# All of batch 1's q turned by transfers, batch 0's k maximum spread by TensorE, the last block of out in 320 and 192 columns, and the queues listed anew

## The chip, the core and the metric

The kernel runs on one core of one Trainium2 chip. The time is the device time of one execution in microseconds (us), the median over runs; less is better. Five engines work beside each other, each through a queue of its own in a fixed order: TensorE (PE, with its weight loads as PEld), VectorE (DVE), ScalarE (ACT), GpSimd (POOL) and SyncE (SP). POOL and SP also issue transfers.

## What is computed

```python
# q, k, v: (8, 8, 576, 64) float32
q_s = softmax(q, axis=-1)            # with max subtracted, 1e-9 added to the sum
k_s = softmax(k, axis=2)             # over the 576 positions, in the same way
kv = np.einsum('bhsd,bhse->bhde', k_s, v)
attn = np.einsum('bhsd,bhde->bhse', q_s, kv)
x = attn.transpose(0, 2, 1, 3).reshape(4608, 512)
a = x @ w1                           # w1, w2: (512, 1024)
b = x @ w2
out = ((a * b) @ w3) @ w_out         # w3: (1024, 1024), w_out: (1024, 512)
```

## The kernel before

**Tiles.** The 128 partitions hold two heads of 64 rows each, and each row has nine tokens (j from 0 to 8); the free dimension holds four such pairs of heads, worked on in two halves (hp 0 and 1). Eight of the nine tokens make the 512 columns of one chunk of x; the ninth tokens of all eight batches are kept in `xtail` and make chunk 8. So there are nine chunks of 512 tokens.

**Folding.** w3 and w_out are multiplied first into one matrix W3O, in eight rows ft. For each ft: `w3t.ft` turns eight 128x128 blocks on TensorE, `w3T.ft` copies them out of PSUM, `pf.ft.0` and `pf.ft.1` are two halves of four matmuls each with the two halves of w_out, and `W3O.ft` copies the result out.

**Attention of batch b.** For k: `kmx` (the maximum over the nine tokens of each partition on DVE, as a tree of four instructions in the first four batches), then `cba`, `cbx`, `cb`, which spread the maximum over the partitions (a transpose of 32x32 blocks and a reduction on DVE, four small copies on ACT, a reduction and a transpose on DVE), then `ksub`, `kexp`, and on TensorE `kv` (with `vc`, a cast of v). `kve` and `kv2` divide by the sums. For q, in parts 0 (tokens 0 to 3) and 1 (tokens 4 to 8): `qmx`, `qsub`, `qexp`, `qsm`, `qeps`, `qrc`, `qn`. Then q has to be turned: on TensorE (`qt`, ten or eight blocks of 128x128, with `qT` to copy them out) or by a transposing transfer on SP (`qd`). Before, batch 0 is turned by TensorE, batch 1 in part 0 by a transfer and in part 1 by TensorE, and the others by transfers. `xm.b.h` and `xt.b` make x on TensorE, `xs` and `xts` copy it out.

**The chunk c.** `up.1` (with w2) and `up.0` (with w1) are eight matmuls of 256 columns, in chunks 0 and 1, or four of 512; `bs` casts the first product, `ab` on DVE multiplies the two; `down.c.tb` are eight matmuls with W3O, `os` copies out, `st` stores. The last block (`down.8.3`) is done in two pieces of columns, so that the end of the work is short.

**The order.** Nothing is scheduled by the compiler. `ORDER` is a list of all steps, and each engine's queue is that list with only its own steps; `PICKS` names the engine where there is a choice. `Plan.run` goes through it, and ties neighbouring steps of DVE and POOL that are marked with `port` to each other (`link`). PSUM has four banks in the ring `pab` (w3t, `up`), two in `po` (`pf`, `down`) and two in `att`; which ring an xm or xt takes, `XRING` says. `FILL` puts matmuls on zeros at the start. The loads in `HW` and `LATE` are issued by SP, those in `LOADS` by POOL, in that order, with a ninth load waiting for the first and so on; the first of `LATE` waits for w1's last quarter, the loads of a batch wait for their buffer, of which there are two.

```python
LOADS = [
    ("w3", 4), ("wo", 0), ("wo", 1), ("w3", 2), ("k", 0), ("w3", 0), ("w3", 3), ("w3", 5),
    ("w3", 1), ("v", 0), ("k", 1), ("w2", 0), ("q", 1, 0), ("w1", 0), ("w2", 1), ("w1", 1),
    ("w1", 2), ("w2", 2), ("k", 2), ("w2", 3), ("w1", 3), ("v", 1), ("q", 1, 1),
]
ROWS = [(0, 1), (1, 2), (2, 3), (3, 4), (4, 6), (6, 8)]   # rows of blocks in one load of w3
```

Of the kernel before, what the change touches and what calls it, by code (L numbers as in the profile page):

```python
# [927 lines left out]
```

## Time and profile before

| | before |
|---|---|
| median of 3 runs | 239.25 us (239.14 to 239.61) |
| the profiled execution | 239.21 us, span 237.4 us |
| TensorE busy | 230.1 us, 97% of the span |
| VectorE, ScalarE, GpSimd busy | 180.3, 121.7, 110.0 us |
| moved by transfers | 46.51 MB, 38.80 MB read from and 9.44 MB written to HBM |

All figures beside the time are of the one profiled execution, whose 239.21 us include 1.8 us around the span of its instructions. A busy TensorE isn't TensorE at its peak: its opening matmuls on zeros count as busy too. The rows of the profile name an instruction by its line in the code, the tile that it writes and those that it reads, and the shapes, with no number of the batch; a step is found by its place in the order.

### The profile page before, as it was taken

Reading aid. Unit: us, or ns where it says so; the run is one execution under the profiler, and the core shown is the slowest. Engines: PE = TensorE matmul, PEld = TensorE weight load, DVE = VectorE, ACT = ScalarE, POOL = GpSimd, SP = SyncE. Lnnn points to the kernel's source line nnn. Section 1 sums busy time; section 2 is a strip of 40 time slices with the busy share of each in tenths; the row PEclk is TensorE's granted clock in tenths of the full one; section 3 lists DMA queues with packets and bytes.
Section 4 is the critical chain, followed back from the end, with each engine's and each line's share of the span. In section 5 each row is a group of like instructions: output and inputs, shape, how many; then the busy total and the mean of one; then the engine's idle time right before and its main releaser. Section 6 shows DMA issues by size and latency. Waiting matters only on the chain.

```text
span 237.4 us, 4860 instructions
## 1 busy us (share of the span) xinstructions
PE 230.1 (97%) x1935; PEld 119.5 (50%) x1935; DVE 180.3 (76%) x277; ACT 121.7 (51%) x221; POOL 110.0 (46%) x73
## 2 busy tenths in 40 slices
...
GB/s 207 214 307 209 306 245 300 328 299 382 401 226 309 405 217 179 385 132 282 242 113 281 387 338 95 51 135 0 3 91 52 0 179 2 32 145 88 3 132 133
DMA packets 38742, 46.51 MB, mean 196 GB/s; under 512 B 17088, under 2 KB 22976, under 8 KB 38720
## 3 DMA queue, kind: packets, MB, share of 16 engines
...
HBM read 38.80 MB, written 9.44 MB: 203 GB/s over the span
## 4 chain that ended last, share of the span: by engine, by line
PE 81%; DMA 8%; DVE 5%; POOL 4%; issue 1%; ACT 0%; POOLq 0%; ACTq 0%
PE pab L784 46%; PE po L806 22%; DMA w<-in_moe_w_dram 6%; PE po L457 4%; PE po L821 3%; PE pkv L549 2%; DMA qT<-en 2%; PE xm L667 1%; DVE qm L582 1%; POOL k L524 1%; PE w3t L445 1%; POOL en L619 1%; POOL w L406 1%; DVE ab L799 1%; DVE kmx L498 1%
## 5 line engine op out<-in xcount | busy, mean ns | idle before, releaser
L784 PE MATMUL pab<-x,w1sb 128*128 128x512 f16 (+1 forms) x320 | 65.9, 337 | 0.4 <-DVE kmx L499 0.4
L784 PE MATMUL pab<-x,w2sb 128*128 128x512 f16 (+1 forms) x320 | 66.0, 337 | 0.0
L799 DVE TENSOR_TENSOR ab<-pab,bsb 128x512 f16<-128x512 f32 x72 | 48.6, 682 | 20.2 <-PE pab L784 13.6
L806 PE MATMUL po<-W3O,ab 128*128 128x512 f16 x256 | 58.9, 379 | 0.0
L784 PEld LDWEIGHTS <-w1sb 128*128 128x128 f16 x352 | 34.2, 98 | 28.5 <-DMA w1sb<-in_moe_w_dram 0.6
L784 PEld LDWEIGHTS <-w2sb 128*128 128x128 f16 x352 | 33.5, 98 | 27.5 <-issue 0.7
L325 ACT CAST bsb<-pab 128x512 f16<-128x512 f32 x46 | 26.8, 582 | 35.8 <-PE pab L784 34.6
L524 POOL TENSOR_TENSOR k<-k,cb 128x1152 f32<-128x1152 f32 x12 | 31.4, 2628 | 16.4 <-issue 5.1
L806 PEld LDWEIGHTS <-ab 128*128 128x128 f16 x256 | 24.5, 98 | 28.5 <-issue 0.4
L587 POOL TENSOR_TENSOR q<-q,qm 128x1024 f32<-128x1024 f32 (+1 forms) x14 | 29.5, 2125 | 13.1 <-DVE rc L573 5.4
L325 ACT COPY osb<-po 128x512 f32<-128x512 f32 (+1 forms) x25 | 14.3, 571 | 40.3 <-PE po L806 26.8
L619 POOL TENSOR_TENSOR en<-eq,qr 128x1024 f16<-128x1024 f16 (+1 forms) x13 | 27.2, 2106 | 10.5 <-DVE qr L612 10.4
L582 DVE TENSOR_REDUCE qm<-q 128x20 f32<-128x1280 f32 (+1 forms) x16 | 21.2, 1340 | 3.6 <-DMA q<-in_q_dram 3.6
L325 DVE CAST bsb<-pab 128x512 f16<-128x512 f32 x26 | 17.6, 677 | 6.8 <-PE pab L784 6.3
L600 DVE TENSOR_REDUCE qr<-eq 128x20 f32<-128x1280 f16 (+1 forms) x16 | 21.5, 1341 | 1.5 <-ACT eq L595 1.4
L595 ACT ACTIVATE eq<-q 128x1280 f16<-128x1280 f32 (+1 forms) x16 | 18.5, 1161 | 4.8 <-DVE q L587 3.9
L532 ACT ACTIVATE ek<-k 128x1152 f16<-128x1152 f32 x16 | 18.2, 1163 | 3.8 <-POOL k L524 3.8
L489 DVE TENSOR_REDUCE km<-k 128x128 f32<-128x1152 f32 x8 | 16.9, 2149 | 0.0
L457 PE MATMUL po<-wosb,w3T 128*128 128x512 f16 x64 | 15.3, 379 | 0.5 <-DMA wosb<-in_moe_w_out_dram 0.5
L325 DVE COPY osb<-po 128x512 f32<-128x512 f32 x12 | 8.3, 688 | 9.1 <-PE po L806 7.9
L329 ACT ACTIVATE x<-xm 128x512 f16<-128x512 f32 x18 | 10.3, 597 | 6.4 <-PE xm L667 6.2
L325 ACT CAST v<-v 128x1152 f16<-128x1152 f32 x9 | 10.3, 1148 | 0.3 <-DMA v<-in_v_dram 0.3
...
## 6 DMA issues: line engine op xcount, KB each, us to landing
...
q<-in_q_dram SPq DMA_DIRECT2D x5, 1152.0 KB, 7.7
v<-in_v_dram SPq DMA_DIRECT2D x5, 1152.0 KB, 8.9
k<-in_k_dram SPq DMA_DIRECT2D x4, 1152.0 KB, 10.1
k<-in_k_dram POOLq DMA_DIRECT2D x3, 1152.0 KB, 14.1
v<-in_v_dram POOLq DMA_DIRECT2D x1, 1152.0 KB, 13.9
v<-in_v_dram SPq DMA_DIRECT2D x2, 576.0 KB, 5.9
q<-in_q_dram SPq DMA_DIRECT2D x2, 576.0 KB, 7.7
```

The source lines that it names most:

```text
L325: return [(nc.scalar.copy if eng == "ACT" else engine[eng].tensor_copy)(out=out, in_=in_)]
L457: nc.tensor.matmul(st["pf", ft], lhsT=st["w3T", ft][:, gt, :], rhs=wosb[:, gt, :], start=(gt == 0), stop=(gt == N_FT - 1))
L524: return [engine[eng].tensor_tensor(out=kb[:, two(hp), :, :], in0=kb[:, two(hp), :, :], in1=st["cb", b][:, two(hp), None, :].broadcast_to( ...
L532: nc.scalar.activation(out=st["ek", b][:, hp, :, :].rearrange("p j (i d) -> p i j d", i=2), in_=kb[:, two(hp), :, :], func=AF.Exp)
L582: dve.tensor_reduce(out=st["qm", b][:, :, j], in_=qb[:, :, j, :], axis=AX.X, op=ALU.max)
L587: return [engine[eng].tensor_tensor(out=qb[:, :, j, :], in0=qb[:, :, j, :], in1=st["qm", b][:, :, j, None].broadcast_to([P, HH, n, D]), op ...
L595: nc.scalar.activation(out=st["eq", b, p], in_=qb[:, :, j, :], func=AF.Exp)
L600: dve.tensor_reduce(out=st["qr", b][:, :, slice(*PARTS[p])], in_=st["eq", b, p], axis=AX.X, op=ALU.add)
L619: return [engine[eng].tensor_tensor(out=st["en", b][:, j, :, :].rearrange("p j h d -> p h j d"), in0=st["eq", b, p], in1=st["qr", b][:, :, ...
L784: nc.tensor.matmul(st["p", one, c, sub, u][:, a * (t1 - t0):(a + 1) * (t1 - t0)], lhsT=w[:, ct, fb * P:(fb + 1) * P], rhs=x()[:, ct, t0:t1 ...
L799: dve.tensor_tensor(out=st["ab", c][:, nf * u:nf * u + nf, t0:t1], in0=cut(st["p", 0, c, sub, u]), in1=cut(st["bsb", c, sub, u]), op=ALU.mult)
L806: nc.tensor.matmul(st["po", c, tb], lhsT=st["ab", c][:, ft, tb * P:(tb + 1) * P], rhs=W3O[:, ft, :], start=(ft == 0), stop=(ft == N_FT - 1))
```

## The change

- `DMATS` 0 and an empty `DMATP`: part 1 of batch 1's q is also turned by a transfer (`qd.1.1`), so `qt.1.8`, `qt.1.16` and their copies `qT` go.
- `PEK = [0]`: in batch 0, `cba`, `cbx` and `cb` are replaced by `kT` (two fp32 transposes of 128x128 on TensorE), `kr` (a reduction on DVE from PSUM) and `kB` (four fp32 matmuls of 128 columns that spread the maximum over the partitions); `ksub.0`, always on DVE, reads the result from PSUM. `ident32` is an identity in fp32, copied by ACT.
- The last block of out is cut at column 320 instead of 256.
- From batch 3 on, `xm.b.0` takes two banks of `pab` instead of `att`.
- q of batch 7 is loaded in one transfer instead of two.
- `ORDER`, `PICKS`, `FILL`, `LOADS` and `LATE` are new lists. q's two normalisations of batch 0 (`qn.0.1`, `qn.0.0`) go from DVE to POOL.
- `CBX` and `KVE` keep what was there for the batches that they name.

The core of the diff, with the order as far as batch 2's first x:

```diff
@@ ORDER @@
-q.0.1 qmx.0.1 qsub.0.1 qexp.0.1 q.0.0 ident w3.4 w3t.5 qmx.0.0 qsm.0.1 wo.0 wo.1 w3.2 k.0 w3.0 w3.3
-w3.5 w3t.4 w3T.5 w3.1 w3T.4 qeps.0.1 qsub.0.0 qrc.0.1 qexp.0.0 qn.0.1 v.0 pf.5.0 pf.4.0 pf.5.1 w3t.2
-qsm.0.0 k.1 w2.0 w3T.2 W3O.5 q.1.0 qt.0.16 qt.0.8 qT.0.8 pf.4.1 qT.0.16 qeps.0.0 qrc.0.0 qn.0.0 w1.0
-pf.2.0 pf.2.1 w3t.0 W3O.2 W3O.4 w3T.0 qt.0.0 w3t.3 pf.0.0 w3T.3 w2.1 pf.0.1 pf.3.0 w3t.7 kmx.0.0
-cba.0 cbx.0 w1.1 pf.3.1 W3O.0 w3T.7 w3t.1 pf.7.0 w3t.6 w1.2 w2.2 cb.0 ksub.0.1 ksub.0.0 kexp.0.1
-kexp.0.0 pf.7.1 qT.0.0 kv.0 W3O.3 w3T.1 W3O.7 kve.0 pf.1.0 pf.1.1 w3T.6 kv2.0 xm.0.0 pf.6.0 pf.6.1
-xs.0.0.1 kmx.1.0 xs.0.0.0 xm.0.1 xs.0.1.0 xs.0.1.1 up.1.0.0.0 bs.0.0.0 xt.0 qmx.1.0 k.2 w2.3 cba.1
-cbx.1 up.0.0.0.0 up.1.0.1.0 up.0.0.1.0 W3O.1 bs.0.1.0 ab.0.0.0 up.1.0.0.1 up.0.0.0.1 w1.3 v.1
-qsub.1.0 qexp.1.0 q.1.1 q.2 xts.0.0 bs.0.0.1 up.1.0.1.1 ab.0.1.0 cb.1 up.0.0.1.1 up.1.0.0.2 qsm.1.0
-ksub.1.1 bs.0.1.1 ab.0.0.1 up.0.0.0.2 up.1.0.1.2 qeps.1.0 xts.0.1 qrc.1.0 qn.1.0 bs.0.0.2 ab.0.1.1
-ab.0.0.2 kmx.2.0 cba.2 bs.0.1.2 kexp.1.1 up.0.0.1.2 up.1.0.0.3 up.0.0.0.3 up.1.0.1.3 bs.0.0.3 W3O.6
-qd.1.0 cbx.2 ab.0.0.3 ksub.1.0 down.0.0 ab.0.1.2 cb.2 vc.1.1 kexp.1.0 vc.1.0 os.0.0 ksub.2.1
-up.0.0.1.3 down.0.1 ksub.2.0 qmx.1.1 qsub.1.1 kv.1 bs.0.1.3 os.0.1 kve.1 kexp.2.1 kexp.2.0 ab.0.1.3
-down.0.2 kv2.1 xm.1.0 down.0.3 xs.1.0.1 xs.1.0.0 up.1.1.0.0 up.0.1.0.0 up.1.1.0.1 qmx.2.1 qmx.2.0
-os.0.2 qsub.2.1 qexp.1.1 bs.1.0.0 qsm.1.1 qsub.2.0 v.2 up.0.1.0.1 up.1.1.0.2 qexp.2.1 ab.1.0.0
-vc.2.1 qeps.1.1 up.0.1.0.2 vc.2.0 qsm.2.1 bs.1.0.1 qexp.2.0 qeps.2.1 kv.2 qrc.1.1 bs.1.0.2 ab.1.0.1
-up.1.1.0.3 up.0.1.0.3 kve.2 ab.1.0.2 qn.1.1 qrc.2.1 kv2.2 qsm.2.0 qt.1.8 os.0.3 qt.1.16 bs.1.0.3
-ab.1.0.3 down.1.0 qeps.2.0 qn.2.1 qrc.2.0 qT.1.16 qT.1.8 xm.1.1 xs.1.1.0 k.3 down.1.1 st.0.0 st.0.1
-q.3 xs.1.1.1 xt.1 xts.1.0 k.4 qd.2.1 qmx.3.0 qmx.3.1 up.1.1.1.0 qn.2.0 bs.1.1.0 xts.1.1 qd.2.0
-kmx.3.0 cba.3 up.0.1.1.0 up.1.1.1.1 up.0.1.1.1 ab.1.1.0 xm.2.0 xs.2.0.0 bs.1.1.1 xs.2.0.1 cbx.3
-ab.1.1.1 cb.3 up.1.1.1.2 up.0.1.1.2 bs.1.1.2 xm.2.1 xs.2.1.0 xs.2.1.1 up.1.1.1.3 up.0.1.1.3 ab.1.1.2
...
+q.0.1 qmx.0.1 q.0.0 qmx.0.0 w3.2 w3.0 wo.0 wo.1 w3.4 qsub.0.1 qexp.0.1 k.0 ident w3t.2 w3T.2 w3t.0
+w3T.0 w3.3 w3.5 pf.2.0 qsm.0.1 qsub.0.0 qexp.0.0 qeps.0.1 qrc.0.1 pf.0.0 pf.2.1 pf.0.1 W3O.0 w3t.4
+q.1.0 qn.0.1 v.0 w3.1 k.1 qsm.0.0 qeps.0.0 qrc.0.0 W3O.2 ident32 qt.0.16 qt.0.8 w3t.5 w3T.4 pf.4.0
+pf.4.1 w3T.5 qT.0.8 W3O.4 pf.5.0 w3t.3 pf.5.1 kmx.0.0 kT.0 kr.0 qT.0.16 w3T.3 pf.3.0 kB.0 w3t.6
+W3O.5 w2.0 w1.0 w3T.6 w3t.7 qn.0.0 w1.1 qt.0.0 ksub.0.1 kexp.0.1 pf.3.1 pf.6.0 pf.6.1 ksub.0.0
+kexp.0.0 qT.0.0 qmx.1.0 kv.0 W3O.6 w3T.7 W3O.3 w3t.1 pf.7.0 kve.0 w2.1 w1.2 w2.2 k.2 qsub.1.0 w3T.1
+kv2.0 xm.0.0 xs.0.0.1 xs.0.0.0 pf.7.1 xm.0.1 pf.1.0 xs.0.1.0 xs.0.1.1 w2.3 w1.3 up.1.0.0.0 v.1 xt.0
+up.0.0.0.0 bs.0.0.0 q.1.1 kmx.1.0 cba.1 cbx.1 qexp.1.0 cb.1 ab.0.0.0 qsm.1.0 xts.0.1 pf.1.1 ksub.1.1
+ksub.1.0 up.1.0.1.0 bs.0.1.0 qeps.1.0 qrc.1.0 W3O.1 up.0.0.1.0 up.1.0.0.1 up.0.0.0.1 bs.0.0.1
+up.1.0.1.1 ab.0.1.0 up.0.0.1.1 ab.0.0.1 bs.0.1.1 up.1.0.0.2 up.0.0.0.2 up.1.0.1.2 kexp.1.0 ab.0.1.1
+bs.0.0.2 kmx.2.0 ab.0.0.2 cba.2 kexp.1.1 xts.0.0 W3O.7 q.2 qn.1.0 up.0.0.1.2 bs.0.1.2 ab.0.1.2
+up.1.0.0.3 up.0.0.0.3 up.1.0.1.3 up.0.0.1.3 bs.0.0.3 ab.0.0.3 down.0.0 cbx.2 cb.2 ksub.2.1 vc.1.0
+vc.1.1 qmx.1.1 bs.0.1.3 kexp.2.1 os.0.0 qd.1.0 kv.1 kve.1 kv2.1 ab.0.1.3 ksub.2.0 qmx.2.1 down.0.1
+down.0.2 os.0.1 qsub.1.1 qexp.1.1 qmx.2.0 xm.1.0 xs.1.0.1 down.0.3 xs.1.0.0 kexp.2.0 qsm.1.1
+qeps.1.1 qsub.2.1 up.1.1.0.0 up.0.1.0.0 up.1.1.0.1 up.0.1.0.1 bs.1.0.0 up.1.1.0.2 qexp.2.1 qsub.2.0
+qrc.1.1 ab.1.0.0 qsm.2.1 qexp.2.0 bs.1.0.1 v.2 k.3 qn.1.1 ab.1.0.1 vc.2.0 vc.2.1 qeps.2.1 qsm.2.0
+os.0.2 os.0.3 st.0.0 q.3 qd.1.1 st.0.1 st.0.2 qrc.2.1 up.0.1.0.2 up.1.1.0.3 kv.2 up.0.1.0.3 qeps.2.0
+bs.1.0.2 ab.1.0.2 qrc.2.0 bs.1.0.3 kve.2 ab.1.0.3 kv2.2 down.1.0 xm.1.1 qmx.3.0 qn.2.1 qn.2.0
+kmx.3.0 cba.3 xs.1.1.1 qsub.3.0 qd.2.1 down.1.1 qd.2.0 xs.1.1.0 qmx.3.1 xt.1 up.1.1.1.0 os.1.0
+os.1.1 xts.1.1 bs.1.1.0 up.0.1.1.0 xts.1.0 cbx.3 up.1.1.1.1 up.0.1.1.1 cb.3 bs.1.1.1 xm.2.0 xs.2.0.1
+qexp.3.0 xs.2.0.0 ab.1.1.0 up.1.1.1.2 up.0.1.1.2 bs.1.1.2 xm.2.1 ab.1.1.1 xs.2.1.0 xs.2.1.1 ab.1.1.2
...
 FILL = {
-    "begin": 17, "pf.5.0": 6,
+    "begin": 14, "pf.2.0": 8,
 }
...
 LOADS = [
-    ("w3", 4), ("wo", 0), ("wo", 1), ("w3", 2), ("k", 0), ("w3", 0), ("w3", 3), ("w3", 5),
-    ("w3", 1), ("v", 0), ("k", 1), ("w2", 0), ("q", 1, 0), ("w1", 0), ("w2", 1), ("w1", 1),
-    ("w1", 2), ("w2", 2), ("k", 2), ("w2", 3), ("w1", 3), ("v", 1), ("q", 1, 1),
+    ("w3", 2), ("w3", 0), ("wo", 0), ("wo", 1), ("w3", 4), ("k", 0), ("w3", 3), ("w3", 5), ("q",
+    1, 0), ("v", 0), ("w3", 1), ("k", 1), ("w2", 0), ("w1", 0), ("w1", 1), ("w2", 1), ("w1", 2),
+    ("w2", 2), ("k", 2), ("w2", 3), ("w1", 3), ("v", 1), ("q", 1, 1),
 ]
 
 
 LATE = [
-    ("q", 2), ("v", 2), ("k", 3), ("q", 3), ("k", 4), ("v", 3), ("q", 4), ("v", 4), ("q", 5),
-    ("k", 5), ("v", 5), ("q", 6), ("k", 6), ("v", 7), ("q", 7), ("v", 6), ("k", 7),
+    ("q", 2), ("v", 2), ("k", 3), ("q", 3), ("k", 4), ("q", 4), ("v", 3), ("v", 4), ("k", 5),
+    ("v", 5), ("q", 5), ("q", 6), ("v", 6), ("k", 6), ("q", 7), ("v", 7), ("k", 7),
 ]
 
 
...
     EPS = 1e-9
     PARTS = [(0, 4), (4, NJ)]
     WOS = 2
-    APART = [("q", 7), ("k", 7), ("v", 7)]
+    APART = [("k", 7), ("v", 7)]
     ROWS = [(0, 1), (1, 2), (2, 3), (3, 4), (4, 6), (6, 8)]
     COLS = [(0, 256), (256, 512), (512, 768), (768, 1024)]
 
...
+    ident32 = konst.tile([P, P], F32)
...
-    DMATS = 1
+    DMATS = 0
     VCASTS = 1
+    PEK = [0]
+    CBX = [1, 2, 3, 4, 5, 6, 7]
+    KVE = [0, 1, 2, 3, 4, 5, 6, 7]
...
-    DMATP = [(1, 0)]
+    DMATP = []
     XMS = 3
     DMAT = [[b > DMATS or (b, p) in DMATP for p in range(2)] for b in range(B)]
...
+    plan.add(("ident32",), "ACT", 0.28, lambda: nc.scalar.copy(out=ident32, in_=ident16), needs=[("ident",)],
+             lead=200.0)
...
+        def kT():
+            st["kT", b] = kbank("kT")
+            for n in range(NHP):
+                nc.tensor.transpose(st["kT", b][:, n, :], st["km", b].rearrange("p h d -> p (h d)")[
+                    :, n * P:(n + 1) * P], ident32)
+
+        def kr():
+            st["kr", b] = work.tile([P, NHP, G], F32, tag="kr", name="kr")
+            dve.tensor_reduce(out=st["kr", b], in_=st["kT", b].rearrange("p n (g r) -> p n g r", g=G),
+                              axis=AX.X, op=ALU.max)
+
+        def kB():
+            st["kB", b] = kbank("kB")
+            for n in range(NHP):
+                for gg in range(G):
+                    nc.tensor.matmul(st["kB", b][gg * HALF:(gg + 1) * HALF, n, :],
+                                     lhsT=st["kr", b][:, n, gg:gg + 1].broadcast_to([P, HALF]),
+                                     rhs=ident32, start=True, stop=True)
+            if not b:
+                st["cb", b] = st["kB", b].rearrange("p n (i d) -> p (n i) d", d=D)
+
...
+        kring = "att" if b else "pab"
+
+        def kbank(name):
+            if b:
+                return p_att([P, NHP, P], F32, name)
+            return pab_pool.tile([P, NHP, P], F32, tag="pab", name=name)
 
...
         def XRING(name):
             if name[1] < XMS:
                 return "att"
-            return "pab" if name[0] == "xt" else "po" if name[2] else "att"
+            return "po" if name[0] == "xm" and name[2] else "pab"
...
         kms = [("kmx", b, hp) for hp in hps if hp == 0 or not TREE[b]]
-        A(("cba", b), "DVE", 0.85, cba, kms)
-        A(("cbx", b), "ACT", 0.5, cbx, [("cba", b)])
-        A(("cb", b), "DVE", 0.62, cb, [("cbx", b)])
+        cbs, cbg = [("cb", b)], []
+        if b in PEK:
+            A(("kT", b), "PE", 0.45, kT, kms + [("ident32",)], takes=kring)
+            A(("kr", b), "DVE", 0.45, kr, [("kT", b)], gives=[("kT", b)])
+            A(("kB", b), "PE", 0.45, kB, [("kr", b)], takes=kring)
+            cbs, cbg = [("kB", b)], [("kB", b)]
+            if b:
+                A(("kc", b), {"ACT": (0.4, False), "DVE": (0.45, False)}, 0, kc, [("kB", b)], gives=[("kB", b)])
+                cbs, cbg = [("kc", b)], []
+        elif b in CBX:
+            A(("cba", b), "DVE", 0.89, cba, kms)
+            A(("cbx", b), "ACT", 0.83, lambda: cbx(True), [("cba", b)])
+            A(("cb", b), "DVE", 0.65, cbz, [("cbx", b)])
+        else:
+            A(("cb", b), "DVE", 2.25, cb, kms)
         for hp in hps:
-            A(("ksub", b, hp), pairs(2 * NJ * D, 2.63), 0, lambda eng, hp=hp: ksub(hp, eng), [("cb", b)])
+            how = {"DVE": (1.35, True)} if b == 0 and cbg else pairs(2 * NJ * D, 2.63)
+            A(("ksub", b, hp), how, 0, lambda eng, hp=hp: ksub(hp, eng), cbs, gives=cbg)
...
-                cuts = [0, C // 2, C] if tb == 3 else [0, C]
+                cuts = [0, 320, C] if tb == 3 else [0, C]
```

128 lines of the change are left out of this document (71 added, 57 removed), and 107 rows, old and new, of the table PICKS.

## The prediction

> **What bounds the kernel now.** I read the page first, then the busy times by stretch, then TensorE's own timeline, and last the issue and landing of the loads.
>
> ```profile
> span 237.4 us, 4860 instructions
> ```
>
> The profiled execution took 239.21 us, 1.8 more than its span, and the median of the runs is 239.25. I add my sum to 239.21, so it speaks of the median within 0.04 us.
>
> The stretches below are cut where TensorE's work changes: the first w3 block arrives at 8.87, the first `up` starts at 33.49, the last eighth of w1 is used at 45.79, batch 2's x starts at 73.37, and the last matmul is issued out at 234.36. Columns: stretch, its length, busy time (and instructions) of PE, PEld, DVE, ACT, POOL, then the granted clock, the DMA share and GB/s.
>
> ```profile
> 8.87:33.49 24.62, 23.52 (x276) 13.02 (x277) 20.51 (x31) 15.26 (x25) 8.75 (x12) 1.00 1.13 266
> 33.49:45.79 12.30, 11.94 (x116) 10.07 (x113) 11.83 (x20) 6.11 (x14) 8.62 (x6) 1.00 1.30 281
> 45.79:73.37 27.58, 27.10 (x346) 18.39 (x347) 25.96 (x42) 20.56 (x37) 20.93 (x10) 1.00 1.03 321
> 73.37:234.36 160.99, 160.98 (x1184) 75.81 (x1184) 117.76 (x178) 77.38 (x144) 65.96 (x32) 1.00 0.56 157
> 234.36:237.40 3.04, 0.00 (x0) 0.00 (x0) 0.00 (x0) 0.37 (x1) 0.00 (x0) 1.00 0.41 144
> ```
>
> After 73.37 TensorE is busy for 160.98 of 160.99 us: only less work or a shorter end gains there, and any new wait is paid in full. Before 73.37 the DMA share is over 1 throughout. So the question is how much of TensorE's work is left at 73.37. Here is its queue up to there (start, length, line, tiles, and the idle time before).
>
> ```profile
> 13.80 1.02 PE L457 MATMUL po<-wosb,w3T 128*128 128x512 f16 x4 [0.50 <-DMA wosb<-in_moe_w_out_dram]
> 15.05 0.71 PE L445 MATMUL w3t<-ident,w 128*128 128x128 f16 x8 [0.23 <-DMA w<-in_moe_w_dram]
> 15.60 0.72 PE L634 MATMUL qtp<-ident,en 128*128 128x128 f16 x10
> 16.16 2.75 PE L457 MATMUL po<-wosb,w3T 128*128 128x512 f16 x12
> ...
> 25.06 0.70 PE L445 MATMUL w3t<-ident,w 128*128 128x128 f16 x8
> 25.59 1.03 PE L457 MATMUL po<-wosb,w3T 128*128 128x512 f16 x4
> 26.46 0.65 PE L445 MATMUL w3t<-ident,w 128*128 128x128 f16 x8
> ...
> 27.90 0.78 PE L549 MATMUL pkv<-v,ek 64*64 64x64 f16 x72
> ...
> 29.14 1.90 PE L457 MATMUL po<-wosb,w3T 128*128 128x512 f16 x8
> 30.97 0.41 PE L667 MATMUL xm<-qT,kv 64*64 64x256 f16 x8
> 31.32 1.90 PE L457 MATMUL po<-wosb,w3T 128*128 128x512 f16 x8
> ...
> 34.66 1.05 PE L784 MATMUL pab<-x,w1sb 128*128 128x256 f16 x8
> ...
> 44.38 1.05 PE L784 MATMUL pab<-x,w2sb 128*128 128x256 f16 x8
> 45.79 1.05 PE L784 MATMUL pab<-x,w1sb 128*128 128x256 f16 x8 [0.36 <-DVE kmx L499]
> ...
> 64.50 0.72 PE L634 MATMUL qtp<-ident,en 128*128 128x128 f16 x10
> 65.06 1.89 PE L806 MATMUL po<-W3O,ab 128*128 128x512 f16 x8
> 66.88 0.41 PE L667 MATMUL xm<-qT,kv 64*64 64x256 f16 x8
> ...
> 73.37 0.41 PE L667 MATMUL xm<-qT,kv 64*64 64x512 f16 x4 [0.46 <-DMA qT<-en]
> ```
>
> Next, loads: for each its issue on POOL, then the row of the transfers' view around that issue, whose last number is the time to landing.
>
> ```profile
> 3.92 0.80 POOL L406 DMA_DIRECT2D k<-in_k_dram  x1
> k<-in_k_dram POOLq DMA_DIRECT2D x1, 1152.0 KB, 14.1
> 11.56 0.75 POOL L406 DMA_DIRECT2D v<-in_v_dram  x1 [1.90 <-DMA wosb<-in_moe_w_out_dram]
> v<-in_v_dram POOLq DMA_DIRECT2D x1, 576.0 KB, 16.2
> 19.36 0.74 POOL L406 DMA_DIRECT2D w1sb<-in_moe_w_dram  x1 [0.34 <-DMA w<-in_moe_w_dram]
> w1sb<-in_moe_w_dram POOLq DMA_DIRECT2D x1, 256.0 KB, 15.1
> 33.52 0.74 POOL L406 DMA_DIRECT2D w1sb<-in_moe_w_dram  x1 [0.62 <-DMA q<-in_q_dram]
> w1sb<-in_moe_w_dram POOLq DMA_DIRECT2D x1, 256.0 KB, 12.2
> ```
>
> So k of batch 0 lands at 18.0, v at 27.8, w1's first quarter at 34.46, and its last at 45.72. TensorE starts the first `up` on w1 at 34.66 and `up.0.0.0.3` at 45.79, 0.2 and 0.07 after those landings: both starts are set by loads, not by the engine that the second row names. The loads land in the order of their list.
>
> **Part by part: the start.** The new list holds the same fourteen loads up to w1's first quarter, and the same twenty-one up to its last, only in another order among themselves. At a DMA share above 1 I leave both landings at 34.46 and 45.72: no gain. POOL now issues them around q's two normalisations, so v of batch 0 is issued near 16 instead of 11.56; it landed 16.2 after its issue because others were ahead of it, some eight of these 16 us are slack, and I price this at nothing too, as I do the one filling matmul that goes before 13.80. What moves is the work of TensorE around them. In the new queue half a fold (`pf.1.1`, four matmuls) comes after `up.0.0.0.0`; all folds were done ahead of it before.
>
> When does the new queue reach `up.0.0.0.0`? The first two w3 pieces and wo come first, w3.4 fifth. From 13.80 to 15.05 one w3 piece of 256 KB arrives, 1.25 us; two such pieces ahead of w3.4 instead of one behind put it at 15.05 + 1.25 = 16.3. What is left from there to `up.1.0.0.0`, which TensorE does nearly without a pause:
> - six blocks of w3 turned, each with half a fold and the gap behind: 1.44 from 26.46 to 27.90, 8.64;
> - five more halves at 0.87 (25.59 to 26.46), 4.35;
> - eighteen blocks of q at 0.056 (ten from 15.60 to 16.16), 1.0;
> - kv.0 from 27.90 to 29.14, 1.24;
> - two xm at 0.35 (30.97 to 31.32) and three gaps of 0.1 (eight matmuls need 1.83 from 29.14 to 30.97, where 8 x 0.216 are 1.73), 1.0;
> - the new fp32 steps kT and kB, six matmuls of 128 columns, which no trace row shows: 0.34 if each costs an f16 block's 0.056, 1.35 at four times that. I take 0.9, nearer the upper end, as each value has twice the bytes.
>
> That is 17.1, and 33.4. Two waits come on top. k of batch 0 has one more w3 piece ahead, 19.2, and its maximum tree takes 2.9 on DVE (rows below), 22.1; TensorE is there at 21.9: 0.2. And `pf.4.0` follows its own eviction closely: 0.4, from 0 to 0.8. So `up.1.0.0.0` at 34.0, and with its 0.87 and xt's 0.3 `up.0.0.0.0` at 35.2, not 34.66. Then `pf.1.1` with its gap, 0.97, and twelve `up`, which took 10.6 from 34.66 to 45.26 (44.38 + 0.88): `up.0.0.0.3` at 46.8, **1.0 later**. If the load alone decides, 34.66 + 0.97 + 10.6 = 46.23, 0.44 later; with the upper prices 1.8 later.
>
> The Trainium skill, FP8 and Floating Point Precision, TensorE Precision Notes, says that true fp32 goes through the array four times; by it kT and kB come to about 1.35 and the sum to 0.45 more. No run here shows it.
>
> DVE and ACT get lighter in that stretch (two normalisations of q go to POOL, and four copies, two transposes and a reduction go away). I price this at nothing: TensorE was busy 23.52 of 24.62 us there, and the loads of w1 bound what follows.
>
> **q of batch 1 by transfers.** Ten blocks leave TensorE: 64.50 to 65.06, **-0.56**, and two evictions leave DVE and ACT, off the path. In their place SP issues one more transposing transfer, behind the load of q.3 and ahead of two stores and batch 2's transposes; k.4 moves behind those, to about 69, and is wanted by DVE only past 80 (nothing). It can start when POOL has normalised the second part.
>
> ```profile
> 60.55 1.14 POOL L325 CAST v<-v 128x1152 f16<-128x1152 f32 x1
> 61.82 6.50 POOL L619 TENSOR_TENSOR en<-eq,qr 128x1280 f16<-128x1280 f16 x3
> DMA to landing us min/median/max: 3.0/3.7/8.2
> ```
>
> The last row is of tile qT: how long such transfers took. The first of the three normalisations (2.3 us) ended at 64.1; the cast ahead of it now comes behind, so 63.0, and qT at 66.7 with the median of 3.7. TensorE reaches `xm.1.1` at 66.88 - 0.56 + 1.0 = 67.3. The cover is 0.6 us; with 8.2 it is 3.9 late. I take **+0.3**.
>
> By the Trainium skill, DMA: Bandwidth & Descriptors, Latency and other measured facts, a transposing DMA moves 261 GB/s, so ten blocks (327,680 bytes) would take an estimated 1.3 us and this term would be nothing. The trace's 3.0 at the least differs and decides.
>
> **The wait at 73.37** (0.46) is for batch 2's qT. TensorE comes 0.44 later and POOL's order ends at the same time: absorbed, **-0.46** (0 if SP's new order delays it as much).
>
> **DVE behind it.**
>
> ```profile
> 68.75 1.21 DVE L498 TENSOR_TENSOR kmx<-k 128x1024 f32<-128x1024 f32 x1
> 71.64 0.45 DVE L505 STREAM_TRANSPOSE kmq<-km 128x256 f32<-128x256 f32 x1
> 72.45 0.68 DVE L799 TENSOR_TENSOR ab<-pab,bsb 128x512 f16<-128x512 f32 x1
> ```
>
> That `ab.1.1.0` stands in the new order behind qmx.3.1, cb.3 and an eviction of xm.2.0 too, some 2.6 us more: it ends near 75, and `up.0.1.1.2`, which takes its bank, is reached near 74.5. **+0.3**, from 0 to 1.2.
>
> **Batches 3 to 7.** Their xm.b.0 takes two of the four pab banks, which `up` needs, where it had banks of its own. The full stretch shows no slack. Each could cost 0 to 0.4; I take **+0.2** in all.
>
> **The end.** Columns 320 and 192 leave TensorE the same columns, but the last eviction is shorter.
>
> ```profile
> L325 ACT COPY osb<-po 128x512 f32<-128x512 f32 x23 | 13.5, 588 | 39.5 <-PE po L806 26.8 <-PE po L821 10.1 <-issue 2.6
> L325 ACT COPY osb<-po 128x256 f32<-128x256 f32 x2 | 0.7, 372 | 0.8 <-PE po L821 0.8
> ```
>
> By these two, 192 columns take about 318 ns, 0.05 less, and the store is a quarter smaller: **-0.1**, 0 to -0.2.
>
> Sum: 1.0 - 0.56 + 0.3 - 0.46 + 0.3 + 0.2 - 0.1 = +0.7. **Forecast 239.9 us**, its own range 239.3 to 240.8.
>
> **Rivals.**
> - *The start stays bound by the load* (faster). If TensorE is at `up.0.0.0.0` by 34.66, as cheap fp32 steps and hidden evictions would allow, and no new wait shows: 0.44 - 0.56 - 0.46 - 0.1 = -0.7, **238.5**. For it: DVE and ACT are lighter in the start. Against it: 17 us of work between 16.3 and 34. It decides from 0.5 us less than my walk. Chance 0.30.
> - *No new wait, but the late start*: 1.0 - 0.56 - 0.46 - 0.1 = -0.1, **239.1**. Chance 0.15.
> - *The new transposing transfer comes late* (much slower). If it takes the 8.2 us of the longest so far, xm.1.1 waits 3.9: 1.0 - 0.56 + 3.9 - 0.46 - 0.1 = +3.8, **243.0**. For it: q.3 is just ahead of it in the same queue. Against it: the median is 3.7. Chance 0.08.
> - *The shared banks bite* in each of five batches at 0.4: 0.7 + 1.8, **241.7**. Chance 0.05.
>
> The forecast has 0.42, of which a quarter falls within 0.2%. That bound, 0.48 us, is about what a measurement of this kernel can tell from no change: 238.77 to 239.73. So faster 0.31, same 0.22, slower 0.47. The range 238.2 to 241.5 leaves out the last two rivals and the outermost of the first.
>
> **What would show it.** In the new profile: `up.0.0.0.0` at 35.2 and `up.0.0.0.3` at 46.8; kT and kB near 0.9 us together; no idle ahead of xm.2.0, at most 0.3 ahead of xm.1.1, some ahead of `up.0.1.1.2`; TensorE full from there on; a final copy near 0.32. Wrong would be: `up.0.0.0.0` at 34.7 (the first rival), w1's last quarter landing at another time than 45.7, or idle TensorE of over 1 us after 75.

## The result, and the profile after

| | before | after | ratio, 95% interval |
|---|---|---|---|
| median of 7 runs each, in turns | 239.61 us | 240.04 us | 1.0025, 1.0013 to 1.0036 |
| the changed kernel once more, on the chip of the last experiments | 239.54 us | 239.90 us | 1.0015, 1.0001 to 1.0028 |
| the profiled execution | 239.21 us, span 237.4 | 240.33 us, span 238.3 | |

The changed kernel is slower by 0.43 us, or by 0.36 us the second time, against the bound of 0.48 us that the prediction named. The two profiled executions lie 1.12 us apart, more than the medians: before's is 0.40 under its median of seven, after's 0.29 over its own. Some 0.2 us of the 1.12 lie outside the span (1.8 us around it before, 2.0 after). What follows names differences between two executions, and each of them carries some 0.3 us of that.

The busy times of the changed kernel by stretch, cut at the same events as before: the first w3 block on TensorE, the first `up`, `up.0.0.0.3`, batch 2's x, the last matmul. Columns as in the prediction.

```profile
7.90:33.78 25.88, 23.91 (x284) 13.46 (x285) 19.32 (x28) 15.24 (x22) 15.19 (x16) 1.00 1.14 264
33.78:46.97 13.19, 12.68 (x118) 10.64 (x117) 10.58 (x19) 8.65 (x19) 7.66 (x6) 1.00 1.27 295
46.97:74.18 27.21, 26.76 (x337) 17.85 (x337) 25.80 (x42) 19.46 (x39) 20.36 (x11) 1.00 1.08 280
74.18:235.30 161.12, 161.12 (x1184) 75.00 (x1184) 114.27 (x171) 74.94 (x142) 69.09 (x34) 1.00 0.58 164
235.30:238.30 3.00, 0.00 (x0) 0.00 (x0) 0.00 (x0) 0.32 (x1) 0.00 (x0) 0.88 0.42 149
```

The full stage is as full as it was and 0.13 us longer. Nearly all of the difference within the span arises ahead of 74.18. TensorE's timeline of the changed kernel there:

```profile
22.52 0.44 PE L547 MATMUL kT<-ident,km 128*128 128x128 f32 x2 [0.23 <-DVE km L513]
22.79 1.03 PE L469 MATMUL po<-wosb,w3T 128*128 128x512 f16 x4
23.75 0.66 PE L559 MATMUL kB<-ident,kr 128*64 128x128 f32 x8
24.34 1.19 PE L457 MATMUL w3t<-ident,w 128*128 128x128 f16 x16
...
34.93 1.05 PE L857 MATMUL pab<-x,w1sb 128*128 128x256 f16 x8
35.82 1.03 PE L469 MATMUL po<-wosb,w3T 128*128 128x512 f16 x4
...
45.41 1.04 PE L857 MATMUL pab<-x,w2sb 128*128 128x256 f16 x8
46.97 1.03 PE L857 MATMUL pab<-x,w1sb 128*128 128x256 f16 x8 [0.52 <-ACT bsb L335]
...
56.04 1.90 PE L879 MATMUL po<-W3O,ab 128*128 128x512 f16 x8
58.07 1.03 PE L857 MATMUL pab<-x,w2sb 128*128 128x256 f16 x8
...
67.82 0.41 PE L725 MATMUL xm<-qT,kv 64*64 64x256 f16 x8
...
74.18 0.41 PE L725 MATMUL xm<-qT,kv 64*64 64x512 f16 x4 [0.33 <-DMA qT<-en]
```

From start to next start, kT takes 0.27 us and kB 0.59. `up.0.0.0.0` starts at 34.93, `up.0.0.0.3` at 46.97, 1.18 later than before, batch 1's x (`xm.1.1`) at 67.82, 0.94 later, batch 2's (`xm.2.0`) at 74.18, 0.81 later. Three waits stand in it.

The first, at 46.97: eight matmuls of 256 columns take 0.87 (44.54 to 45.41 in the same view), so TensorE was there at 45.41 + 0.87 = 46.28. The last quarter of w1 was issued at 33.59 and landed 12.5 later, 46.09. What was missing was a PSUM bank. The row names a cast on ACT, `bs.0.1.2`. ACT's timeline has it behind two exponentials of k and two other evictions; it is the first of the two in the last row, took 0.60 and ended at 46.92, 0.05 ahead of the matmul:

```profile
43.08 1.17 ACT L586 ACTIVATE ek<-k 128x1152 f16<-128x1152 f32 x1 [1.25 <-DMA w2sb<-in_moe_w_dram]
44.16 0.57 ACT L335 CAST bsb<-pab 128x512 f16<-128x512 f32 x1
44.62 1.16 ACT L586 ACTIVATE ek<-k 128x1152 f16<-128x1152 f32 x1
45.69 0.27 ACT L339 ACTIVATE xtail<-xt 128x128 f16<-128x128 f32 x1
45.84 0.60 ACT L339 ACTIVATE W3O<-po 128x512 f16<-128x512 f32 x1
46.32 1.08 ACT L335 CAST bsb<-pab 128x512 f16<-128x512 f32 x2
```

The bank that had been in use longest is the one that `ab.0.0.2` empties. DVE's timeline has that step behind the maximum tree of batch 2, and it ended at 46.50 + 0.69 = 47.19, after the matmul had begun:

```profile
43.56 1.23 DVE L510 TENSOR_TENSOR kmx<-k 128x1024 f32<-128x1024 f32 x1 [0.68 <-DMA k<-in_k_dram]
...
46.01 0.43 DVE L513 TENSOR_TENSOR km<-kmx,k 128x256 f32<-128x256 f32 x1
46.50 0.69 DVE L872 TENSOR_TENSOR ab<-pab,bsb 128x512 f16<-128x512 f32 x1
```

Before, `ab.0.0.2` came ahead of this tree. So TensorE waits 0.69 us for a bank from two engines that were called lighter: DVE frees none before 47.19, as its tree waits for a load of k, and ACT, with its queue full, frees the next at 46.92.

The second, at 58.07: `down.0.3` ends at 56.04 + 1.73 = 57.77. ACT has an exponential of q (`qexp.1.1`) ahead of the eviction of x (`xs.1.0.0`), and it waits for POOL's subtraction:

```profile
56.26 1.27 ACT L653 ACTIVATE eq<-q 128x1280 f16<-128x1280 f32 x1 [1.60 <-POOL q L645]
57.44 0.58 ACT L339 ACTIVATE x<-xm 128x512 f16<-128x512 f32 x1
```

The third, at 74.18, is for batch 2's transposing transfers. POOL's and SP's timelines, and the end of the chain of waits there:

```profile
64.19 4.20 POOL L677 TENSOR_TENSOR en<-eq,qr 128x1280 f16<-128x1280 f16 x2 [0.40 <-DVE qr L670]
```

```profile
62.72 1.80 SPq L700 DMA_TRANSPOSE qT<-en  x1
64.56 3.20 SPq L905 DMA_DIRECT2D out_dram<-osb  x4
67.87 2.84 SPq L700 DMA_TRANSPOSE qT<-en  x2
```

```profile
68.40 0.78 SPq L700
69.18 0.05 issue
69.23 0.02 SPq L700
69.25 0.03 issue
69.28 4.76 DMA qT<-en
74.04 0.14 issue
74.18 0.41 PE xm L725 x4
```

POOL had the second source ready at 68.39, as before (68.32). But SP's queue holds the new transfer `qd.1.1` and four stores first and needs 5 us to issue them (62.72 to 67.76), so the transfer that `xm.2.0` needs went out at 69.28, 0.9 behind its source. It landed 4.76 us after that; before, the same transfer went out at 68.35 and landed 4.89 later.

### The profile page after: what moved, and what is told of

It reads as the page before. It is cut to its first block, busy times and chain, and to the rows that moved or that the text cites. A ratio compares the mean times of both kernels' runs of the same rounds, so it can differ in the third digit from the quotient of the medians.

```text
span 238.3 us, 4853 instructions
## 1 busy us (share of the span) xinstructions
PE 229.6 (96%) x1934; PEld 118.7 (50%) x1934; DVE 172.6 (72%) x263; ACT 119.9 (50%) x222; POOL 118.1 (50%) x78
## 2 busy tenths in 40 slices
DMA packets 40038, 46.84 MB, mean 197 GB/s; under 512 B 18384, under 2 KB 24272, under 8 KB 40016
## 4 chain that ended last, share of the span: by engine, by line
PE 72%; DMA 14%; POOL 4%; DVE 3%; issue 3%; ACT 2%; SPq 0%; DVEq 0%; POOLq 0%; ACTq 0%
PE pab L857 46%; PE po L879 19%; DMA k<-in_k_dram 12%; PE po L894 3%; DMA qT<-en 2%; PE pkv L603 2%; POOL k L578 1%; DVE kmx L510 1%; POOL q L645 1%; PE pab L725 1%; POOL w L416 1%; POOL en L677 1%; DVE kmx L511 1%; ACT eq L653 1%; PE po L725 1%
## 5 line engine op out<-in xcount | busy, mean ns | idle before, releaser
L335 ACT CAST bsb<-pab 128x512 f16<-128x512 f32 x49 | 28.3, 584 | 53.9 <-PE pab L857 53.7
L677 POOL TENSOR_TENSOR en<-eq,qr 128x1280 f16<-128x1280 f16 (+1 forms) x15 | 31.9, 2137 | 24.7 <-DVE qr L670 15.5
L335 ACT COPY osb<-po 128x512 f32<-128x512 f32 (+1 forms) x28 | 15.9, 578 | 14.5 <-PE po L879 8.1
L335 DVE CAST bsb<-pab 128x512 f16<-128x512 f32 x23 | 15.7, 683 | 4.4 <-PE pab L857 3.9
L335 DVE COPY osb<-po 128x512 f32<-128x512 f32 (+1 forms) x9 | 6.0, 664 | 15.6 <-PE po L879 10.8
L469 PEld LDWEIGHTS <-w3T 128*128 128x128 f16 x64 | 5.9, 98 | 7.0 <-issue 1.7
L335 POOL CAST v<-v 128x1152 f16<-128x1152 f32 x8 | 9.1, 1148 | 0.0
```

The source lines that it names most:

```text
L335: return [(nc.scalar.copy if eng == "ACT" else engine[eng].tensor_copy)(out=out, in_=in_)]
L469: nc.tensor.matmul(st["pf", ft], lhsT=st["w3T", ft][:, gt, :], rhs=wosb[:, gt, :], start=(gt == 0), stop=(gt == N_FT - 1))
L677: return [engine[eng].tensor_tensor(out=st["en", b][:, j, :, :].rearrange("p j h d -> p h j d"), in0=st["eq", b, p], in1=st["qr", b][:, :, ...
```

## The experiments

Two theories were set against each other. A: what ends last ahead of the full stage is the chain to batch 2's q, and TensorE's delays ahead of it are free. B: TensorE's queue, each wait paid in full. All ran in five rounds beside the kernel before, which had medians of 239.50 (e), 239.48 (f1 to f4) and 239.54 (the last four).

| run | median us | ratio to before, 95% | xm.2.0 at |
|---|---|---|---|
| e1_no_bank_wait | 239.62 | 1.0006, 0.9995 to 1.0017 | 73.59 |
| e2_stores_behind | 242.71 | 1.0136, 1.0109 to 1.0163 | 75.24 |
| e4_blocks_back | 241.36 | 1.0080, 1.0067 to 1.0093 | 75.42 |
| e5_no_fp32 | 239.67 | 1.0008, 0.9998 to 1.0019 | 73.49 |
| f1_x_first | 240.13 | 1.0027, 1.0018 to 1.0036 | 74.21 |
| f2_three_waits | 239.37 | 0.9995, 0.9984 to 1.0007 | 73.17 |
| f3_q2_sooner | 239.38 | 1.0001, 0.9989 to 1.0013 | 72.91 |
| f4_no_fp32 | 239.78 | 1.0014, 1.0003 to 1.0025 | 74.47 |
| c_again | 239.90 | 1.0015, 1.0001 to 1.0028 | 74.33 |
| f5_att_banks | 241.75 | 1.0094, 1.0075 to 1.0112 | 74.09 |
| f6_blocks_uncovered | 239.54 | 1.0004, 0.9993 to 1.0015 | 73.53 |
| g_best | 240.81 | 1.0068, 1.0042 to 1.0095 | 73.01 |

**e1: the bank wait.**

```diff
-bs.0.0.2 kmx.2.0 ab.0.0.2 cba.2 kexp.1.1 ... up.0.0.1.2 bs.0.1.2 ab.0.1.2
-up.1.0.0.3 up.0.0.0.3 up.1.0.1.3 up.0.0.1.3 bs.0.0.3 ab.0.0.3 down.0.0 cbx.2
+bs.0.0.2 kmx.2.0 ab.0.0.2 kmy.2 cba.2 kexp.1.1 ... up.0.0.1.2 bs.0.1.2
+up.1.0.0.3 up.0.0.0.3 bs.0.0.3 ab.0.0.3 up.1.0.1.3 down.0.0 ab.0.1.2 up.0.0.1.3 cbx.2
...
+            one = [top(out=t, in0=kb[:, :, 0:4, :], in1=kb[:, :, 4:8, :], op=ALU.max)]
+            return one if b == 2 else one + kmy()
```

> The changed kernel, with the wait ahead of up.0.0.0.3 taken away: batch 2's maximum tree (kmx.2.0) is cut behind its first instruction and ab.0.0.2 goes between the two pieces; ab.0.0.3 and down.0.0 go ahead of ab.0.1.2 and up.0.0.1.3, so that no later wait takes its place. Theory A (what ends last ahead of the full stage is the second transposing transfer of batch 2's q, landed at 74.04; TensorE's own delays ahead of it are free): up.0.0.0.3 starts at 46.3 instead of 46.97, but xm.2.0 still at 74.1 to 74.3 behind a wait of about 1.0 instead of 0.33, and the median stays at 240.0. Theory B (TensorE's queue: each of its waits is paid in full): xm.2.0 near 73.5, the median 239.4.

No idle time is left ahead of `up.0.0.0.3`, which starts at 46.15, though ACT's cast of `bs.0.1.2` ends as late as it did (46.84): DVE's order is enough. The second wait took most of it back, `up.1.1.0.0` is only 0.18 earlier:

```profile
57.89 1.03 PE L865 MATMUL pab<-x,w2sb 128*128 128x256 f16 x8 [0.72 <-ACT x L339]
...
73.59 0.41 PE L730 MATMUL xm<-qT,kv 64*64 64x512 f16 x4
```

The median fell by 0.19% against the changed kernel's first ratio, 0.4 us, and by 0.09% against its second, 0.2 us, between A's nothing and B's 0.6. A named the wrong place: it was ACT's order at 57.9 that gave the gain back, not the transfer at 74. In this execution SP was through its stores sooner (both transposing transfers out from 67.07) and no wait for qT shows; `xm.2.0` is where B had it, the median is not, so neither theory held as it stood.

**e2: the stores behind the transfers.** Only SP's queue changes.

```diff
-os.0.2 os.0.3 st.0.0 q.3 qd.1.1 st.0.1 st.0.2 qrc.2.1
+os.0.2 os.0.3 st.0.0 q.3 qd.1.1 qrc.2.1
...
-qd.2.1 down.1.1 qd.2.0 xs.1.1.0
+qd.2.1 down.1.1 qd.2.0 st.0.1 st.0.2 xs.1.1.0
```

> The changed kernel, with the four stores of blocks 0.1 and 0.2 moved behind the two transposing transfers of batch 2's q in SP's queue, nothing else. In the changed kernel SP issued the first of the two at 67.87, behind those stores (its source was normalised near 66.5), and the second at 69.28 (its source was ready at 68.39). Theory A (that transfer ends last): the second is issued near 68.5, lands near 73.3, xm.2.0 starts at 73.85 with no wait, the median goes to 239.7. Theory B (a transposing transfer's time is set by the traffic beside it, not by its issue): landing stays near 74.0, the median at 240.0.

Both missed: 2.7 us slower than the changed kernel. ACT's and TensorE's timelines:

```profile
74.42 0.58 ACT L335 COPY osb<-po 128x512 f32<-128x512 f32 x1 [4.76 <-DMA out_dram<-osb]
```

```profile
75.24 0.40 PE L725 MATMUL xm<-qT,kv 64*64 64x512 f16 x2 [1.57 <-ACT xtail L339]
```

There are four output buffers. The eviction `os.1.1` needs that of `st.0.1`; it stood 4.76 us on ACT, and the evictions of xtail, which free the banks of `xm.2.0`, stood behind it. The edit made a wait of its own, so the median says nothing on the transfers. The trace does: with the stores behind, the second transfer went out at 68.28, as A said, and landed after 3.11 us, at 71.38, where A had 73.3 and B 74.0. Of the stores only `st.0.2` can move, as f2 does.

**e4: the ten blocks back on TensorE.** The copies go to DVE (`qT.1.16`) and ACT (`qT.1.8`).

```diff
-    DMATS = 0
-    DMATP = []
+    DMATS = 1
+    DMATP = [(1, 0)]
...
-st.0.0 q.3 qd.1.1 st.0.1
+st.0.0 q.3 st.0.1
...
-ab.1.0.3 kv2.2 down.1.0 xm.1.1 qmx.3.0
+ab.1.0.3 kv2.2 qt.1.8 qt.1.16 down.1.0 qT.1.16 qT.1.8 xm.1.1 qmx.3.0
```

> The changed kernel, with part 1 of batch 1's q turned by TensorE again as before (ten blocks of 128x128 ahead of down.1.0, copied out by DVE and ACT), and its transposing transfer gone. Theory A (TensorE has only 0.33 us of cover ahead of batch 2's x): the 0.56 us of blocks move xm.2.0 to 74.4, the median is 240.2 to 240.3. Theory B (every block counts): 240.6. Theory C (the added transfer disturbs the others in its queue): batch 2's transfers land earlier without it and the median is at or below 240.0.

```profile
67.07 0.73 PE L692 MATMUL qtp<-ident,en 128*128 128x128 f16 x10 [1.27 <-DVE kv L633]
```

The blocks take their banks from att, which in this order `kv.2` holds until DVE's `kv2.2`: 1.27 of waiting and 0.57 of blocks. That is again the edit's own wait; f6 mends it. C is borne out as far as the transfers go: without the added one, batch 2's second went out at 68.16 and landed at 71.26.

**e5: no fp32 on TensorE.** The three old steps take the place of the three new ones.

```diff
-    PEK = [0]
-    CBX = [1, 2, 3, 4, 5, 6, 7]
+    PEK = []
+    CBX = [0, 1, 2, 3, 4, 5, 6, 7]
...
-pf.5.1 kmx.0.0 kT.0 kr.0 qT.0.16 w3T.3 pf.3.0 kB.0 w3t.6 W3O.5 w2.0
+pf.5.1 kmx.0.0 cba.0 qT.0.16 w3T.3 pf.3.0 w3t.6 W3O.5 cbx.0 cb.0 w2.0
```

> The changed kernel, with batch 0's maximum of k spread by DVE and ACT as before (cba, cbx, cb) and no fp32 steps on TensorE. Theory A: TensorE loses 0.86 us of work ahead of the first up, which then starts with w1's first quarter near 34.6 instead of 34.93; what follows is held by the bank of up.0.0.0.3 at 46.97 and by batch 2's q at 74.04, so xm.2.0 stays at 74.1 to 74.2 and the median at 240.0. Theory B (the start is TensorE's work): up.0.0.0.0 near 34.1, the median 239.2 to 239.5. Theory C (the maximum comes late without TensorE): kv.0 waits up to 1 us and the median is above 240.3.

`up.0.0.0.0` came at 35.15, not sooner: kv.0 waits for its exponential and starts 21.02 us after the first w3 block, where it took 20.60 in the changed kernel. B is out: the 0.86 us of TensorE's work that went away came back as waiting (0.63 of it ahead of kv.0), since the maximum comes later on DVE and ACT in this order. That is C's mechanism, though not C's median, and A's 34.6 missed. The median is nevertheless 0.17% lower than the changed kernel's first ratio and 0.07% lower than its second; this execution, with SP's list unchanged, shows no wait at `xm.2.0`, where A had it held by batch 2's q.

**f1: x ahead of the exponential on ACT.** One step moves.

```diff
-qsub.1.1 qexp.1.1 qmx.2.0 xm.1.0 xs.1.0.1 down.0.3 xs.1.0.0 kexp.2.0
+qsub.1.1 qmx.2.0 xm.1.0 xs.1.0.1 down.0.3 xs.1.0.0 qexp.1.1 kexp.2.0
```

> The changed kernel, with ACT's exponential of batch 1's q, part 1 (qexp.1.1), moved behind xs.1.0.0, as before the change; nothing else. In the changed kernel and in three of the four runs so far ACT did this exponential first, which waits for POOL's subtraction near 56.0 to 56.2, and TensorE's up.1.1.0.0 started at 57.8 to 58.1 whatever came ahead of it. Theory A (this order on ACT is a wall that hides what the start loses): up.1.1.0.0 follows down.0.3 without a gap, near 57.7 to 57.8 and 0.1 to 0.3 earlier, the median 239.8 to 239.9. Theory B (the exponential is itself on the chain to batch 2's q): qn.1.1 ends 0.2 to 0.4 later, xm.2.0 waits for it, the median at 240.0 to 240.3.

```profile
74.21 0.41 PE L725 MATMUL xm<-qT,kv 64*64 64x512 f16 x4 [0.71 <-DMA qT<-en]
```

`up.1.1.0.0` came without a gap (57.76), as A said, and the whole of it was lost at 74.21, so the median is B's. POOL waited 0.81 for batch 2's reciprocal where it had waited 0.40.

**f2: all three waits.** The edits of e1 and f1, and:

```diff
-st.0.0 q.3 qd.1.1 st.0.1 st.0.2 qrc.2.1
+st.0.0 q.3 qd.1.1 st.0.1 qrc.2.1
...
-qd.2.1 down.1.1 qd.2.0 xs.1.1.0
+qd.2.1 down.1.1 qd.2.0 st.0.2 xs.1.1.0
```

> The kernel without the bank wait (e1), with xs.1.0.0 ahead of qexp.1.1 too, and with the two stores of block 0.2 alone moved behind batch 2's two transposing transfers (not those of block 0.1, whose buffer the next block needs). Without them up.1.1.0.0 would start near 57.2 (0.72 earlier than in e1) and xm.1.1 near 66.9. Theory A (the transfers of q then end last): a wait of 0.2 to 0.5 shows ahead of xm.1.1 or xm.2.0, since qT of part 1 lands near 67.2 and that of batch 2 near 73.2; xm.2.0 at 73.1 to 73.3, the median 239.3. Theory B (TensorE's queue alone): no wait, xm.2.0 at 72.9, the median 238.9.

```profile
66.50 3.10 SPq L705 DMA_TRANSPOSE qT<-en  x2
```

```profile
73.17 0.41 PE L730 MATMUL xm<-qT,kv 64*64 64x512 f16 x4
```

With two of the four stores in front, the pair went out from 66.50 instead of 67.87, and the second transfer, out at 68.37, landed after 3.1 us. TensorE reached batch 2's x 1.0 us sooner than in the changed kernel and found it there: B in the trace. The median gained 0.3% on the changed kernel's first ratio, 0.7 us (0.2%, 0.5 us, on its second), and stands where A put it. It is the kernel before's time. The profiled execution is 0.58 above this median, and shows one place where it lost time later: batch 3's x waited for a transposing transfer too, which landed 6.9 us after its issue.

```profile
92.77 0.41 PE L730 MATMUL pab<-qT,kv 64*64 64x512 f16 x4 [0.34 <-DMA qT<-en]
```

**f3: batch 2's normalisation sooner.** On top of f2:

```diff
-ab.1.0.1 vc.2.0 vc.2.1 qeps.2.1 qsm.2.0 os.0.2
+ab.1.0.1 vc.2.0 qeps.2.1 vc.2.1 qrc.2.1 qsm.2.0 os.0.2
```

> The kernel of f2, with batch 2's normalisation brought forward: qeps.2.1 ahead of the cast vc.2.1 on ACT and qrc.2.1 ahead of qsm.2.0 on DVE, which takes away the 0.4 us for which POOL waited for that reciprocal. Theory A: batch 2's second transposing transfer is issued and lands 0.3 to 0.4 earlier, near 72.9, xm.2.0 at 72.9 to 73.1, the median 0.1 to 0.3 under f2's. Theory B (TensorE's queue or xm.1.1's transfer ends last): no difference from f2.

POOL's wait is gone (its two normalisations end at 67.66), and the median is f2's: B. TensorE runs without an idle row from 22.2 to its end, so in this execution (0.31 under the median) no idle time behind 23 us is left to take away, only work.

**f4: f3 without fp32 on TensorE.** The diff of e5 on f3.

> The kernel of f3, with no fp32 steps on TensorE (batch 0's maximum of k spread by DVE and ACT, as in e5). With the waits behind it gone, this tells what the fp32 steps cost where nothing covers them. Theory A (the fp32 steps bring k's maximum to kv.0 sooner by what they cost): up.0.0.0.0 within 0.3 of f3's, the median within 0.2 of f3's. Theory B (0.86 us of TensorE's work): 0.86 under f3's.

```profile
29.18 0.78 PE L608 MATMUL pkv<-v,ek 64*64 64x64 f16 x72 [0.89 <-ACT ek L591]
...
68.50 0.41 PE L730 MATMUL xm<-qT,kv 64*64 64x256 f16 x8 [0.62 <-DMA qT<-en]
```

A's mechanism, and more of it than A said: all that TensorE saved is spent waiting for k's exponential, and `up.0.0.0.0` came 0.95 later than in f3. The median is 0.4 over f3's, where e5's was 0.4 under the changed kernel's, both at the edge of their intervals. So the steps' own price is not told from nothing; that taking them out in this order does not gain 0.86 is shown twice. The second row is the wait that the prediction priced at +0.3, seen here for the first time, in an execution 0.57 above its median.

**c_again: the changed kernel once more,** without an edit.

> The changed kernel itself, once more and on the same chip as the three beside it: its profile so far was of an execution 0.3 us above the median. Theory A (the wait ahead of batch 2's x is the rule): xm.2.0 waits 0.3 to 0.7 for its transfer, 0.25% over the kernel before. Theory B (it was that execution's alone): no wait there, and 0.1% over the kernel before, as for the kernel without fp32 steps.

```profile
74.33 0.41 PE L725 MATMUL xm<-qT,kv 64*64 64x512 f16 x4 [0.60 <-DMA qT<-en]
```

A for this kernel: both of its profiles have the wait. Of the six profiles with SP's list as in the changed kernel, four (this one, the first, f1, f5) have 0.33 to 0.71 of waiting at `xm.2.0`, and there SP is through the four stores at 67.6 to 67.8. In the other two, e1 and e5, it is through at 67.0 and 67.1, and there is no wait. The ratio is between the two expectations.

**f5: batches 3 to 7 back in att's banks.** The copies `xts` move so that the banks are free in the order of the list.

```diff
-            return "po" if name[0] == "xm" and name[2] else "pab"
+            return "pab" if name[0] == "xt" else "po" if name[2] else "att"
...
-cb.4 xm.3.0 xm.3.1
+cb.4 xts.2.0 xts.2.1 xm.3.0 xm.3.1
```

> The changed kernel with xm.b.0 of batches 3 to 7 in att's two banks again instead of two of pab (and xtail's two copies of batch 2 ahead of xm.3.0, which makes that possible). From xm.2.0 to the last block TensorE took 153.88 us before the change and 154.03 in the changed kernel and in three of its variants. Theory A (the shared banks cost it): 153.85 to 153.95, the median 0.15 lower. Theory B (the new places of xt and xm in the order cost it, by more changes between kinds of matmul): 154.03, the median unchanged.

```profile
93.76 0.40 PE L725 MATMUL xm<-qT,kv 64*64 64x512 f16 x2 [0.41 <-ACT xtail L339]
94.85 0.40 PE L725 MATMUL xm<-qT,kv 64*64 64x512 f16 x2 [0.69 <-ACT x L339]
```

Neither. In this order `xt.2` and `kv.3` hold att, and `xm.3.0` waits for it twice: the stage is 1.7 us longer. That is the edit's own wait, so what pab's banks cost is not told by it; in the changed kernel no idle row stands in that stage. From `xm.2.0` to the first matmul of the last chunk (`down.8.0`) the changed kernel, c_again, e1, e4, e5, f1, f3, f4 and f6 take 153.98 to 154.08 against 153.88 in the one trace of the kernel before (154.69 in f2, with the wait shown there). So the 0.15 is likely real, but its cause stays open.

**f6: the ten blocks where no wait covers them.** On f3, `DMATS` and `DMATP` as in e4, no `qd.1.1`, and:

```diff
-qsm.2.0 os.0.2 os.0.3 st.0.0
+qsm.2.0 st.0.0
...
-up.0.1.0.2 up.1.1.0.3 kv.2 up.0.1.0.3 qeps.2.0 bs.1.0.2 ab.1.0.2 qrc.2.0 bs.1.0.3 kve.2 ab.1.0.3
+up.0.1.0.2 qt.1.8 qt.1.16 qT.1.16 qT.1.8 up.1.1.0.3 up.0.1.0.3 kv.2 qeps.2.0 bs.1.0.2 ab.1.0.2 qrc.2.0
+os.0.2 bs.1.0.3 kve.2 os.0.3 ab.1.0.3
```

> The kernel of f3, in which no wait shows on TensorE from 23 us on, with part 1 of batch 1's q turned by TensorE again, this time ahead of up.1.1.0.3, kv.2 behind up.0.1.0.3 and the copies os.0.2 and os.0.3 later, so that no bank is waited for. Theory A (TensorE's work counts in full where nothing covers it): xm.2.0 0.5 to 0.6 later than in f3, the median 239.9. Theory B (something else ends last there): less than 0.3 later, the median under 239.7.

```profile
73.53 0.41 PE L730 MATMUL xm<-qT,kv 64*64 64x512 f16 x4
```

In the two traces `xm.2.0` is 0.62 later than in f3, as A says: 0.56 of blocks. But the median is under B's 239.7: the two are 0.16 apart, and their intervals overlap. Twelve executions of f3 spread from 239.06 to 240.04, those of f6 from 239.38 to 239.69 but for one at 240.03. So the exchange may be worth its 0.6 in f3's best executions and less in the median; that the transfer in place of the blocks brings the spread would fit, but was not tried by itself, and f2's wait at 92.77 is another candidate.

**g: f3 with f5's banks,** the two diffs together.

> The kernel of f3 with the bank change of f5: every edit that took away a wait, and the shorter full stage if f5 shows one. Theory A: f3's 239.4 less 0.15, so 239.2, 0.1% under the kernel before, at the edge of what can be told from it. Theory B (the banks cost nothing): 239.4, no difference from the kernel before.

`xm.3.0` waits as in f5, 1.4 us lost. No version found beats the kernel before: f2 and f3 equal it. The new lists of loads, the filling matmuls and q's single load of batch 7 were not tried by themselves.

## Why the prediction was right, and where its steps were not

The forecast was +0.7 on 239.21, 239.9; measured were 240.04 and 239.90, a difference of +0.43 and +0.36. The level agreed partly because the execution that the sum was added to was 0.40 under the later median; on that median the same sum would have given 240.3. The sum itself was some 0.3 too large, and its terms fit less well than their total: ahead of `xm.2.0` they add up to +0.28 where the trace has +0.81, behind it to +0.4 where the trace has about +0.05. That the two errors nearly cancelled is luck.

| step | forecast | found in the trace |
|---|---|---|
| `up.0.0.0.0`, `up.0.0.0.3` | 35.2, 46.8: +1.0 | 34.93, 46.97: +1.18 |
| kT and kB | 0.9 together | 0.86 |
| wait at `xm.1.1` for the new transfer | +0.3 | none (0.62 in f4) |
| ten blocks gone | -0.56 | gone; 0.62 between f6 and f3 |
| wait at 73.37 | -0.46, absorbed | 0.33 and 0.60 are left in the kernel's two profiles |
| `up.0.1.1.2` behind `ab.1.1.0` | +0.3 | none |
| batches 3 to 7 | +0.2 for shared banks | +0.15, no idle row; cause open |
| end | -0.1 | -0.1 |
| a wait at `up.1.1.0.0` | not seen | 0.30, and 0.72 in e1 |

*The start.* The walk through TensorE's queue put `up.0.0.0.0` 0.27 too late: of the two waits added, k's is there (0.23) and `pf.4.0`'s 0.4 is not. The half fold behind `up.0.0.0.0` cost what was said. The step that failed is "I price this at nothing" for DVE and ACT: the order puts `kmx.2.0` ahead of `ab.0.0.2`, which ties a bank to the landing of k, and `kexp.1.1` ahead of `bs.0.1.2`, which holds back the next bank. Without that TensorE would have started at 46.28, half a microsecond under the forecast; with it, 0.69 later, it came to 46.97 against 46.8. Two errors cancelled. One of the prediction's own signs of being wrong came, w1's last quarter landed at 46.09 and not at 45.7, but TensorE was not there before 46.28.

*The new transfer.* Its source was ready at 62.69 (forecast 63.0), it went out at 62.72 and landed 4.7 later, 67.42, while TensorE came at 67.82, 0.30 of it from the second wait. The mechanism was right and the arrival off by half a microsecond; f4, where TensorE came at 67.9 and the data 0.6 later, shows the price in one execution.

*The wait at 73.37.* It was to be absorbed, "0 if SP's new order delays it as much". It does: the added transfer and the stores behind it take SP 5 us. This is the step where the list had been read and the time of SP's own issues had not been added up. f2, with two of the four stores in front, has no wait. But the time of issue is only part of it. In the four profiles where batch 2's second transfer went out past 69.1 (the changed kernel, c_again, f1, f5) it landed 4.76 to 4.94 us later; in the nine where it went out by 68.7, 3.04 to 3.26 later. So 0.6 us of issue, from e5's 68.66 to 69.28, became 2.1 at the landing, 71.91 against 74.04. Why is not shown, and the kernel before, with 68.35 and 4.89, does not fit that line.

*DVE behind it.* `ab.1.1.0` started at 75.22, later than forecast, and yet `up.0.1.1.2` followed the matmuls ahead of it at 75.40 without a gap, some 0.5 before `ab.1.1.0` ended. So "which takes its bank" was wrong, as at 46.97: the matmul took another bank than that of `ab.1.1.0`.

*The end* did as it said: from the start of `down.8.0` to the end of the span 10.19 became 10.08, and 10.06 to 10.14 in the other runs; the last copy takes 0.32, as forecast.

```profile
235.38 0.32 ACT L335 COPY osb<-po 128x192 f32<-128x192 f32 x1 [1.16 <-PE po L894]
```

The rival "the load bounds the start" missed where TensorE was 0.35 behind w1's first quarter (19.78 + 14.8 = 34.58), and the half fold followed. The rivals on a late transfer (3.9 us) and on shared banks (0.4 in each batch) did not come.
